# Deeper look-ahead and moved gradient blocks ahead of a backward loop

## The chip, the cores and the metric

The kernel runs on one core of a Trainium2 chip. The metric is the time of one execution in device microseconds. Seven executions of the kernel before took 5657.28 to 5668.17 us, with a median of 5661.39 us.

## What is computed

The reference is one training step, forward and backward, of a block with a memory-augmented attention (A) and a gated feed-forward part (B):

```
xn = layernorm(x)                      # x: 2048 tokens of 640
s  = A(xn);  g = silu(B(xn));  out = x + s * g
A: mem = mem0                          # 8 rows
   for each of 64 segments of 32 tokens:
       h = [mem ; xs]                  # 40 rows
       q, k, v = h Wq, h Wk, h Wv      # 32 heads of 128
       p = softmax(mask(q k^T / sqrt(128)));  o = (p v) Wo
       mem = o[:8];  out rows = o[8:]
B: out = (silu(x w1) * (x w3)) w2
```

The outputs are `out` and the gradients of x, mem0 and the seven weights for a given `grad_out`. All arrays are bf16. The memory rows link the segments, so the forward pass of A is a chain of 64 steps, and the backward pass is a chain of 64 steps in the other direction, from step 63 to step 0.

## The kernel before

The kernel is a sequence of stages that pass their data through scratch tensors in HBM. The ones that matter here are the end of the forward pass of A, the output stage, and the beginning of its backward pass.

**Tiles and units.** Three segments make one tile: 24 memory rows and 96 token rows, 120 in all. There are 22 tiles; the last (tile 21) holds one segment, 8 + 32 = 40 rows. A unit is one tile and four heads (`qd`, 512 columns), so a tile has eight units.

**phase3b_out (L814, the output stage).** It multiplies the attention's rows with Wo (`ld`, `turn`, `proj`, L834 to L865). Its work is 32 turns, four blocks of eight: two blocks of three tiles, then tile 20, then tile 21. In a turn, the rows of the turn four later are loaded (`orow`, five buffers, on SP's queue), the next turn's rows are transposed on PE, and this turn's are multiplied. Two other things ride along. The first is `fetch` (L822 to L826, issued at L920): 13 loads of weights that the backward pass needs, five of 1 MB (WoT) and eight of 1.28 MB (WvT and WkT), one a turn on SP's queue behind the turn's row load. The second is `gox` (L894): gradient units. One such unit takes 128 tokens of the scaled output gradient (`g0x`, loaded from GST) and makes 512 columns of their product with WoT: five matmuls of 512 columns into one PSUM bank, a copy to SBUF (DVE for even units, ACT for odd ones), and after every second unit a store of 128 x 1024 to the scratch tensor GX0 from ACT's queue. GX0 holds tokens 1344 to 2047, so there are six blocks of eight units, 48 in all, from the last token block to the first. They are taken from turn 7 on, one a turn in the first two blocks of turns and three a turn after that.

**phase4_Abwd (L960, the backward pass).** For each unit it has six functions. `ld` (L1131) loads a unit's q and v rows (`gqv`: the memory rows of q and of v in one or two pieces each, and the token rows of both), its output gradients (`gor`, from GX0 for tiles 14 to 21), and its probabilities (`gPr`). `turn` transposes v and the gradients on PE, copies them out on ACT (`gvT`, two buffers, and `gOT`) and stores gvT to VTD from POOL's queue. `dprob` multiplies the two. `dsoft` makes the softmax gradient on DVE (`gdS`) and stores it to DSR from POOL's queue. `gmem` multiplies for the keys and values of the memory rows, copies on ACT (`gks`) and stores to GXP from SP's queue. `gmem_ld` is `gmem` followed by the load of a further unit.

The lead-in (L1256 to L1271) runs 19 units ahead of the first step: the eight of tile 21 (40 rows, called small below), the eight of tile 20 and three of tile 19 (120 rows, called big). It is a software pipeline: iteration i does `turn` of unit i, `dprob` and `dsoft` of unit i-1, and `gmem_ld` of unit i-2. Four loads go out ahead of it, into four buffers, so the load behind `gmem` of unit i-2 is that of unit i+2. `gor` and `gPr` are issued from ACT's queue, the rest from SP's. In iterations 1, 4, 7 and 10 POOL issues a quarter of WqT, 1.28 MB each. The last four loads are those of units that belong to the steps. At the end SP issues the loads of step 63 (vTt, gPm, Qst, krow, xp, gride), and POOL copies gride into the input of the step's first matmuls (L1003).

Then `chain(t)` runs for t = 63 to 0, with the remaining units of the tiles placed into its gaps by hand.

**What sets the order.** Both stages end with `in_order`, which makes every engine keep the order in which the program wrote its instructions. An instruction that waits therefore holds up all that is written behind it on its engine or queue. DMAs are issued by SP, ACT and POOL, each with a queue of its own.

Of the kernel before, what the change touches and what calls it, by code (L numbers as in the profile page):

```python
# [9 lines left out]
BF16 = mybir.dt.bfloat16  # L10
F32 = mybir.dt.float32
# [5 lines left out]
P = 128  # L17
# [23 lines left out]
class K:  # L41
# [110 lines left out]
    def setup_dram(self):  # L152
        tc = self.tc
        S, D, T, H, F = self.S, self.D, self.T, self.H, self.F
        HD = self.HD
        dp = self.ctx.enter_context(tc.tile_pool(name="scratch", bufs=1, space=bass.MemoryType.DRAM))
        self.dp = dp
        mk = lambda name, shape, dt=BF16: dp.tile(list(shape), dt, name=name, uniquify=False)
        self.XN = mk("XN", (S, D))
        self.XNT = mk("XNT", (D, S))  # L160
        self.SLT = mk("SLT", (F, S))
        self.DUT = mk("DUT", (F, S))
        self.HB = mk("HB", (S, F))
# [24 lines left out]
        self.GB0 = 1344  # L188
        self.GX0 = mk("GX0", (S - self.GB0, HD))
# [621 lines left out]
    return Wo  # L811


def phase3b_out(k, Wo, W0, W4):  # L814


    nc, tc = k.nc, k.tc
    D, DC, H, HD, T = k.D, k.DC, k.H, k.HD, k.T
    WT = {}
    WoT = W0.tile([P, DC, HD], BF16, name="WoT", tag="w0")  # L820
    src = k.WOT.rearrange("(dc p) j -> p dc j", p=P)
    fetch = [(WoT[:, dc], src[:, dc]) for dc in range(DC)]  # L822
    for (nm_, src, tag) in (("v", k.WVT, "w1"), ("k", k.WKT, "w2")):
        WT[nm_] = W4.tile([P, H, D], BF16, name=f"W{nm_}T", tag=tag)
        src = src.rearrange("(h p) d -> p h d", p=P)
        fetch += [(WT[nm_][:, h0:h0 + 8], src[:, h0:h0 + 8]) for h0 in range(0, H, 8)]  # L826
    with tc.tile_pool(name="oio", bufs=1) as io, tc.tile_pool(name="oac", bufs=1, space=bass.MemoryType.PSUM) as pa, \
# [5 lines left out]
        st, acc = {}, {}  # L833
# [49 lines left out]
            nc.scalar.dma_start(k.SR[96 * (tl + t):96 * (tl + t) + nx, :], s_tok[0:nx, :])  # L883


        g0 = [(x0, cg, b) for x0 in range(k.GB0, k.S, P)[::-1] for cg in range(4) for b in range(2)]

        def gox_ld(x0):
            w = min(P, k.S - x0)
            xs = io.tile([P, DC, P], BF16, name="g0x", tag="g0x", bufs=2)  # L890
            nc.scalar.dma_start(xs[:, :, 0:w], k.GST[:, x0:x0 + w].rearrange("(dc p) t -> p dc t", p=P))
            st["gx", x0] = xs

        def gox(x0, cg, b):  # L894
            w = min(P, k.S - x0)
            if cg == 0 and b == 0 and x0 > k.GB0:
# [3 lines left out]
            xs, sg = st["gx", x0], st["gs"]  # L900
            c0 = cg * 1024 + b * 512
            pb = ps.tile([P, 512], F32, name="g0pb", tag="opt")
            for dc in range(DC):
                nc.tensor.matmul(pb[0:w, :], xs[:, dc, 0:w], WoT[:, dc, c0:c0 + 512], start=(dc == 0), stop=(dc == DC - 1))
            k.copy(sg[0:w, b * 512:(b + 1) * 512], pb[0:w, :], eng='vs'[b])
            if b == 1:
                nc.scalar.dma_start(k.GX0[x0 - k.GB0:x0 - k.GB0 + w, cg * 1024:(cg + 1) * 1024], sg[0:w, :])

        start = len(nc.cur_bb.bb.instructions)
        assert g0[0][0] - g0[-1][0] == P * (len(g0) // 8 - 1)  # L910
# [5 lines left out]
        for i, (b, qd) in enumerate(work):  # L916
            if i + 4 < len(work):
                ld(*work[i + 4])
            if fetch:
                nc.sync.dma_start(*fetch.pop(0))  # L920
            if i + 1 < len(work):
                turn(*work[i + 1])
            proj(b, qd)
            if late:
                rows_out(*late.pop(0))
            if qd == 7:
                ep_a(b)
# [14 lines left out]
    for s in range(3):  # L942
        t0 = (2, 0, 1)[s]
        n = (T - 1 - t0 + 2) // 3
# [15 lines left out]
def phase4_Abwd(k, out2, WoT, WvT, WkT, WqT, later):  # L960
    nc, tc = k.nc, k.tc
    D, DC, S, H, HD, T = k.D, k.DC, k.S, k.H, k.HD, k.T
    out2f = out2.flatten_outer_dims()
    with tc.tile_pool(name="gst", bufs=1) as st, tc.tile_pool(name="gchain", bufs=1) as ch, \
# [3 lines left out]
        NG = 4  # L968
# [234 lines left out]
        start = len(nc.cur_bb.bb.instructions)  # L1203
# [3 lines left out]
        pro = [(tl, qd) for tl in (k.NTL - 1, k.NTL - 2) for qd in range(8)] + parts[0]  # L1207
        batch = {}
        for i, p in enumerate(parts[1:]):
            batch[T - 2 - i] = p  # L1210

        todo = [u for t in range(T - 1, -1, -1) for u in batch.get(t, ())]

        def ld_next():
            if todo:
                n0 = len(pro) - (total - len(todo))
                ld(*todo.pop(0), nc.scalar if n0 > 0 else nc.sync)

        def gmem_ld(tl, qd):
            gmem(tl, qd)  # L1220
            ld_next()
# [35 lines left out]
        total = len(todo)  # L1257
        for _ in range(4):
            ld_next()
        for i in range(len(pro) + 2):  # L1260
            for f, o in ((turn, 0), (dprob, 1), (dsoft, 1), (gmem_ld, 2)):
                if 0 <= i - o < len(pro):
                    f(*pro[i - o])
            if i % 3 == 1 and i < 12:
                h0 = 8 * (i // 3)
                nc.gpsimd.dma_start(WqT[:, h0:h0 + 8], k.WQT.rearrange("(h p) d -> p h d", p=P)[:, h0:h0 + 8])
        loads(T - 1)
        load_k(T - 1)
        load_xp(T - 1)
# [677 lines left out]
```

## Time and profile before

| what | value |
|---|---|
| median of 7 executions | 5661.39 us |
| the profiled execution | 5668.17 us, the slowest of the seven |
| its span in the profile | 5666.5 us |
| PE busy over the span | 5037.3 us, 89% |
| DVE, ACT, POOL busy | 42%, 32%, 27% |
| output stage, rows first loaded to last matmul | 1981.8 to 2118.2 us |
| lead-in, first load issued to step 63's input copied | 2120.7 to 2227.3 us |

How to read it: the profile lists busy time by engine and cuts the span into slices. PE is the matmul engine and PEld its weight loads; PEclk, or the granted clock, is the share of full speed at which PE ran. A group line names a source line, an engine, an operation, the tile written and the tiles read, and how often. A line of waits says which instruction stood idle, what released it, for how long in total, how many times and the longest. A timeline line has a start, a length, the engine, the line, the operation and its count, and in brackets the idle time ahead of it with what ended it. An engine name with a q is its queue that issues DMAs.

### The profile page before, as it was taken

The numbers are of one execution on the slowest core, as the hardware profiler recorded it, in microseconds if no ns is written. First come the engines' busy times: TensorE is split into PE (matmuls) and PEld (weight loads), VectorE is DVE, ScalarE is ACT, GpSimd is POOL, SyncE is SP. The second block draws the span as 40 slices with busy tenths as digits, with TensorE's granted clock in tenths as the row PEclk, the third lists the DMA queues.
The fourth block names the chain that finished last, engine by engine and source line by source line (L and its number), as shares of the span: only waits on it lengthen the run. The fifth ranks groups of instructions, "written<-read, shape, count | busy, mean of one in ns | idle before, by whom it ended". The sixth has DMA issues, their size and how long they took to land. (4 is left out here: it accounts for less than half of the span.)

```text
span 5666.5 us, 167048 instructions
## 1 busy us (share of the span) xinstructions
PE 5037.3 (89%) x67614; PEld 3209.4 (57%) x67614; DVE 2388.0 (42%) x7479; ACT 1835.4 (32%) x5045; POOL 1551.3 (27%) x2576
## 2 busy tenths in 40 slices
PE   5959799999999784999999997999999999999999
PEld 2536455555555453565556654665566556657565
DVE  5824455555555423444444442332233223311451
ACT  2424355555555522333333331332233122301111
POOL 0000144444444302333333332332234223300000
PEclk9969899999999796999999998999999999999999
DMA  6565355555555475666666664543344334456332
GB/s 219 167 243 197 114 156 160 156 160 160 157 151 149 107 207 155 172 176 175 183 173 178 177 172 108 134 96 93 80 118 99 96 86 106 119 165 227 101 117 91
DMA packets 1009114, 835.81 MB, mean 148 GB/s; under 512 B 506462, under 2 KB 895874, under 8 KB 1005028
## 3 DMA queue, kind: packets, MB, share of 16 engines
q1 hardware_dynamic: 759999, 574.71, 36.6%
q0 software_dynamic: 90352, 141.70, 8.9%
q10 hardware_dynamic: 157993, 108.73, 6.7%
q8 instruction: 533, 8.73, 0.7%
q14 instruction: 237, 1.94, 0.1%
HBM read 511.81 MB, written 324.39 MB: 148 GB/s over the span
## 5 line engine op out<-in xcount | busy, mean ns | idle before, releaser
L1409 PE MATMUL wg<-gr,hr 120*128 120x512 bf16 (+1 forms) x2640 | 591.6, 385 | 17.6 <-DVE dST L1341 13.1
L1387 PE MATMUL g<-w,gT 128*128 128x320 bf16 x3840 | 547.8, 299 | 0.0
L1409 PEld LDWEIGHTS <-hr 120*128 120x128 bf16 (+1 forms) x2640 | 258.5, 99 | 342.6 <-issue 50.7
L1387 PEld LDWEIGHTS <-gT 128*128 128x128 bf16 x3840 | 368.6, 98 | 136.0
L250 POOL DMA_DIRECT2D r<-GOS x256 | 143.4, 564 | 792.3 <-PE r6p L1351 749.4
L373 PEld LDWEIGHTS <-gkv 128*8 128x8 bf16 x8192 | 217.7, 100 | 159.7 <-DVE gkv L1048 35.0
L90 DVE CAST wgo<-wg 128x512 bf16<-128x512 f32 x72 | 47.5, 687 | 586.6 <-PE wg L1409 294.0
L354 PEld LDWEIGHTS <-hx 128*32 128x32 bf16 x7680 | 177.6, 96 | 164.0 <-issue 3.3
L373 PE MATMUL gbank<-WvT,gkv 128*8 128x320 bf16 x4096 | 236.5, 410 | 28.0 <-DVE gkv L1048 28.0
L90 DVE CAST stg<-bank 128x512 bf16<-128x512 f32 x256 | 176.9, 691 | 199.6 <-PE bank L354 188.8
L663 ACT ACTIVATE xP<-xsp,xnm 120x120 bf16<-120x120 f32 (+1 forms) x704 | 239.9, 375 | 10.4 <-DVE xnm L659 5.2
L1396 DVE TENSOR_TENSOR ghacc<-ghacc,g 128x320 f32<-128x320 f32 x240 | 116.9, 487 | 277.1 <-PE g L1387 277.1
L92 ACT CAST wgo<-wg 128x512 bf16<-128x512 f32 x48 | 25.8, 589 | 639.2 <-PE wg L1409 639.2
L1354 ACT CAST gr<-r6p 120x512 bf16<-120x512 f32 (+1 forms) x176 | 103.1, 586 | 351.4 <-PE r6p L1351 337.9
L1185 POOL DMA_DIRECT2D DSR<-gdS x176 | 100.5, 571 | 409.1 <-DVE gdS L1183 386.8
L92 ACT COPY gT<-t6g 128x960 bf16<-128x960 bf16 (+5 forms) x216 | 166.8, 792 | 128.0 <-PE t6g L1370 127.6
L712 POOL DMA_DIRECT2D OR<-xv x163 | 94.1, 577 | 407.5 <-ACT xv L711 290.2
L674 POOL TENSOR_TENSOR xP<-xP,xrz 120x480 bf16<-120x480 bf16 x163 | 161.7, 992 | 140.1 <-ACT xP L663 91.0
L1183 DVE SCALAR_TENSOR_TENSOR gdS<-gdp,Dx,gPr 120x120 bf16<-120x120 f32 (+1 forms) x704 | 188.6, 329 | 0.0
L1180 DVE CUSTOM_DVE_ANT_0 gdS<-gdp,gPr 120x120 bf16<-120x120 f32 (+1 forms) x704 | 153.6, 273 | 65.2 <-PE gdp L1169 54.8
L1155 POOL DMA_DIRECT2D VTD<-gvT x176 | 129.3, 738 | 180.2 <-ACT gvT L1154 155.7
L1370 PE MATMUL t6g<-ident,gr 120*128 120x120 bf16 (+1 forms) x2112 | 172.3, 221 | 3.3 <-DVE wgo L90 2.7
(340 smaller groups left out, 11218.0 us busy)
## 6 DMA issues: line engine op xcount, KB each, us to landing
QVS<-stg SPq DMA_DIRECT2D x128, 256.0 KB
gqv<-QVS SPq DMA_DIRECT2D x112, 192.0 KB
vTt<-VTD SPq DMA_DIRECT2D x64, 320.0 KB
VTD<-gvT POOLq DMA_DIRECT2D x168, 120.0 KB, 3.4
OR<-xv POOLq DMA_DIRECT2D x163, 120.0 KB, 2.6
DSR<-gdS POOLq DMA_DIRECT2D x168, 112.5 KB, 3.3
dS<-DSR SPq DMA_DIRECT2D x168, 112.5 KB
P<-PR SPq DMA_DIRECT2D x168, 112.5 KB
```

The lines of the kernel that those rows point to most:

```text
L90: return nc.vector.tensor_copy(out, in_)
L92: return nc.scalar.copy(out, in_)
L250: eng.dma_start(d, src if src.shape[0] > 1 else src[0])
L354: k.nc.tensor.matmul(bank[32 * g:32 * g + 32, :], x[:, dc, :], W[:, dc, c0:c0 + 512], start=(dc == 0), stop=(dc == k.DC - 1), tile_positio ...
L373: k.nc.tensor.matmul(pm[p0:p0 + nq, 0:320], x[:, h, :], W[:, h, 320 * b:320 * b + 320], start=(first and i == 0), stop=(last and i == 15), ...
L663: nc.scalar.activation(Pb[0:n, j, 0:n], sp[0:n, j, :], ACT.Exp, bias=nmx[0:n, j:j + 1], scale=k.scale, accum_out=Z[0:n, j:j + 1])
L674: eng.tensor_tensor(Pb[0:n, :, 0:n], Pb[0:n, :, 0:n], bc_last(rz[0:n], n), ALU.mult)
L1180: nc.vector.tensor_tensor_reduce(dS[0:n, j, :], dp[0:n, j, :], Pr[0:n, j, :], 1.0, 0.0, ALU.mult, ALU.add, Dx[0:n, j:j + 1])
L1183: nc.vector.scalar_tensor_tensor(dS[0:n, j, :], dp[0:n, j, :], Dx[0:n, j:j + 1], Pr[0:n, j, :], op0=ALU.subtract, op1=ALU.mult)
L1370: nc.tensor.transpose(pt[:, i - i0, j, :], st["g", u, i][0:n, j * P:(j + 1) * P], k.ident[0:n, 0:n])
L1387: nc.tensor.matmul(pg[:], ring[:, i, j, r0:r0 + P], Ws[qd][i][:, j, 320 * h:320 * h + 320], start=(i == 0 and j == 0), stop=(i == 2 and j ...
L1409: nc.tensor.matmul(accs[dc][:], hr[0:n, tl, dc * P:(dc + 1) * P], st["g", NTL * qd + tl, i][0:n, :], start=(tl == 0), stop=(tl == NTL - 1))
```

## The change

Three things are changed; the rest of the program is as it was, apart from line numbers.

The first is in the output stage. The last two blocks of gradient units (tokens 1344 to 1599, 16 units) are not made there; 32 units remain. And of the 13 weight fetches the first five still go out one a turn, but the other eight only in every third turn: turns 6, 9, 12, 15, 18, 21, 24 and 27.

The second is the loads of the lead-in. Six go out ahead instead of four. Units whose number is 4 or 5 modulo 6 use a new buffer pair, `xb`, in SBUF that `krow` of step 63 takes later; the others use the four buffers of before. So the load behind `gmem` of unit i-2 is that of unit i+4. In the lead-in the memory rows of v are issued from POOL's queue, `gor` from ACT's queue for units after the fourth and from SP's before, and `gPr` from SP's queue. The last four loads, which belong to the steps, stand at the last four iterations, as before.

The third is where the 16 units went: one at the end of each iteration 1 to 16 of the lead-in, after that iteration's WqT fetch if it has one. They use the banks bA and bB, which the steps use later; the block load (at the first of eight units, right before its matmuls, in the one buffer that `xp` takes later) and the stores (one buffer, that of `gstg`) are on POOL's queue.

```diff
+def gx_ld(k, xs, x0, eng):
+    w = min(P, k.S - x0)
+    eng.dma_start(xs[:, :, 0:w], k.GST[:, x0:x0 + w].rearrange("(dc p) t -> p dc t", p=P))
+
+def gx_block(k, xs, sg, pb, WoT, x0, cg, b, eng):
+    w = min(P, k.S - x0)
+    c0 = cg * 1024 + b * 512
+    for dc in range(k.DC):
+        k.nc.tensor.matmul(pb[0:w, :], xs[:, dc, 0:w], WoT[:, dc, c0:c0 + 512], start=(dc == 0), stop=(dc == k.DC - 1))
+    k.copy(sg[0:w, b * 512:(b + 1) * 512], pb[0:w, :], eng='vs'[b])
+    if b == 1:
+        eng.dma_start(k.GX0[x0 - k.GB0:x0 - k.GB0 + w, cg * 1024:(cg + 1) * 1024], sg[0:w, :])
...
-        g0 = [(x0, cg, b) for x0 in range(k.GB0, k.S, P)[::-1] for cg in range(4) for b in range(2)]
+        g0 = [(x0, cg, b) for x0 in range(k.GB0 + k.GL, k.S, P)[::-1] for cg in range(4) for b in range(2)]
...
-            if fetch:
+            if fetch and (len(fetch) > 8 or i % 3 == 0):
                 nc.sync.dma_start(*fetch.pop(0))
...
-        def ld(tl, qd, eng=nc.sync):
+        def ld(tl, qd, eng=None):
             ns, nm, nx, n = k.geo(tl)
             c0, h0 = qd * 512, qd * 4
-            qv = fl.tile([120, 2, 512], BF16, name="gqv", tag="gqv", bufs=4)
-            k.load_m(qv, tl, "qv", c0, c0 + 512, nc.sync)
+            i = cnt["l"]
+            cnt["l"] += 1
+            early = i < len(pro)
+            g = i % 6 if early else (i - len(pro) + 1) % NG
+            if g < NG:
+                gor = gors[g][:]
+                qv = fl.tile([120, 2, 512], BF16, name="gqv", tag="gqv", bufs=4)[:]
+                Pr = fl.tile([120, 4, n], BF16, name="gPr", tag="gPr", bufs=4)[:]
+            else:
+                x = xb[:, g - NG]
+                qv = x[:, 0:1024].rearrange("p (i c) -> p i c", i=2)
+                gor = x[:, 1024:1536]
+                Pr = x[:, 1536:1536 + 4 * n].rearrange("p (h c) -> p h c", h=4)
+            if gnm.get(g, 0 if g < NG else 1) != 0 and (g >= NG or gnm[g] < nm):
+                nc.vector.memset(gor[0:24, :], 0.0)
+            gnm[g] = nm
+            for (a, b, src, w) in k.m_src(tl, "qv", c0, c0 + 512):
+                (nc.gpsimd if early and w else nc.sync).dma_start(qv[a:b, w], src if src.shape[0] > 1 else src[0])
             k.load_x(qv, nm, k.x_src(tl, "qv", c0, c0 + 512), nc.sync)
-            gor = gors[qd % NG]
-            if tl == k.NTL - 2 and qd < NG:
-                nc.vector.memset(gor[0:24, :], 0.0)
-            k.load_x(gor, nm, k.g_src(tl, c0, c0 + 512), eng)
-            Pr = fl.tile([120, 4, n], BF16, name="gPr", tag="gPr", bufs=4)
-            eng.dma_start(Pr[0:n], k.PR[tl][:, h0:h0 + 4, :])
+            k.load_x(gor, nm, k.g_src(tl, c0, c0 + 512), nc.scalar if early and i > 3 else nc.sync)
+            nc.sync.dma_start(Pr[0:n], k.PR[tl][:, h0:h0 + 4, :])
...
+        xb = ch.tile([120, 2, 2048], BF16, name="xb", tag="krow", bufs=1)
+        g0 = [(x0, cg, b) for x0 in range(k.GB0, k.GB0 + k.GL, P)[::-1] for cg in range(4) for b in range(2)]
+
+        def gox(x0, cg, b):
+            if cg == 0 and b == 0:
+                uu["gx"] = ch.tile([P, DC, P], BF16, name="gx0", tag="xp", bufs=1)
+                gx_ld(k, uu["gx"], x0, nc.gpsimd)
+            if b == 0:
+                uu["gs"] = ch.tile([P, 1024], BF16, name="gstg", tag="gstg", bufs=1)
+            gx_block(k, uu["gx"], uu["gs"], (bA, bB)[b], WoT, x0, cg, b, nc.gpsimd)
+
-        for _ in range(4):
+        for _ in range(6):
             ld_next()
         for i in range(len(pro) + 2):
-            for f, o in ((turn, 0), (dprob, 1), (dsoft, 1), (gmem_ld, 2)):
+            for f, o in ((turn, 0), (dprob, 1), (dsoft, 1), (gmem, 2)):
                 if 0 <= i - o < len(pro):
                     f(*pro[i - o])
+            if 0 <= i - 2 and (i - 2 + 6 < len(pro) or i >= len(pro) - 2):
+                ld_next()
             if i % 3 == 1 and i < 12:
                 h0 = 8 * (i // 3)
                 nc.gpsimd.dma_start(WqT[:, h0:h0 + 8], k.WQT.rearrange("(h p) d -> p h d", p=P)[:, h0:h0 + 8])
+            if g0 and i > 0:
+                gox(*g0.pop(0))
```

`GB0` is 1344 and `GL` is 256. The output stage's own `gox` calls `gx_ld` and `gx_block` with ACT's queue.

More of the change, by code (lines that the diff above doesn't have):

```diff
@@ L188, in setup_dram @@
         self.GB0 = 1344
+        self.GL = 2 * P
         self.GX0 = mk("GX0", (S - self.GB0, HD))
@@ L883, in rows_out @@
             nc.scalar.dma_start(k.SR[96 * (tl + t):96 * (tl + t) + nx, :], s_tok[0:nx, :])
-        g0 = [(x0, cg, b) for x0 in range(k.GB0, k.S, P)[::-1] for cg in range(4) for b in range(2)]
+        g0 = [(x0, cg, b) for x0 in range(k.GB0 + k.GL, k.S, P)[::-1] for cg in range(4) for b in range(2)]
         def gox_ld(x0):
-            w = min(P, k.S - x0)
             xs = io.tile([P, DC, P], BF16, name="g0x", tag="g0x", bufs=2)
-            nc.scalar.dma_start(xs[:, :, 0:w], k.GST[:, x0:x0 + w].rearrange("(dc p) t -> p dc t", p=P))
+            gx_ld(k, xs, x0, nc.scalar)
             st["gx", x0] = xs
         def gox(x0, cg, b):
-            w = min(P, k.S - x0)
-            if cg == 0 and b == 0 and x0 > k.GB0:
+            if cg == 0 and b == 0 and x0 > k.GB0 + k.GL:
                 gox_ld(x0 - P)
@@ L899, in gox @@
                 st["gs"] = io.tile([P, 1024], BF16, name="g0st", tag="g0st", bufs=3)
[L900 to L907, printed above, removed]
+            gx_block(k, st["gx", x0], st["gs"], ps.tile([P, 512], F32, name="g0pb", tag="opt"), WoT, x0, cg, b, nc.scalar)
         start = len(nc.cur_bb.bb.instructions)
@@ L1129, in phase4_Abwd @@
         uu = {}
-        def ld(tl, qd, eng=nc.sync):
+        gnm = {}
+        def ld(tl, qd, eng=None):
             ns, nm, nx, n = k.geo(tl)
             c0, h0 = qd * 512, qd * 4
-            qv = fl.tile([120, 2, 512], BF16, name="gqv", tag="gqv", bufs=4)
-            k.load_m(qv, tl, "qv", c0, c0 + 512, nc.sync)
-            k.load_x(qv, nm, k.x_src(tl, "qv", c0, c0 + 512), nc.sync)
-            gor = gors[qd % NG]
-            if tl == k.NTL - 2 and qd < NG:
-                nc.vector.memset(gor[0:24, :], 0.0)
-            k.load_x(gor, nm, k.g_src(tl, c0, c0 + 512), eng)
-            Pr = fl.tile([120, 4, n], BF16, name="gPr", tag="gPr", bufs=4)
-            eng.dma_start(Pr[0:n], k.PR[tl][:, h0:h0 + 4, :])
+            i = cnt["l"]
[16 more added lines that the diff above has]
+                (nc.gpsimd if early and w else nc.sync).dma_start(qv[a:b, w], src if src.shape[0] > 1 else src[0])
+            k.load_x(qv, nm, k.x_src(tl, "qv", c0, c0 + 512), nc.sync)
+            k.load_x(gor, nm, k.g_src(tl, c0, c0 + 512), nc.scalar if early and i > 3 else nc.sync)
+            nc.sync.dma_start(Pr[0:n], k.PR[tl][:, h0:h0 + 4, :])
             uu["l", tl, qd] = qv, gor, Pr
@@ L1210, in phase4_Abwd @@
             batch[T - 2 - i] = p
+        cnt = dict(l=0)
         todo = [u for t in range(T - 1, -1, -1) for u in batch.get(t, ())]
@@ L1215, in ld_next @@
             if todo:
-                n0 = len(pro) - (total - len(todo))
-                ld(*todo.pop(0), nc.scalar if n0 > 0 else nc.sync)
+                ld(*todo.pop(0))
         def gmem_ld(tl, qd):
@@ L1256, in phase4_Abwd @@
         todo = pro + todo
-        total = len(todo)
-        for _ in range(4):
+        xb = ch.tile([120, 2, 2048], BF16, name="xb", tag="krow", bufs=1)
[8 more added lines that the diff above has]
+        for _ in range(6):
             ld_next()
         for i in range(len(pro) + 2):
-            for f, o in ((turn, 0), (dprob, 1), (dsoft, 1), (gmem_ld, 2)):
+            for f, o in ((turn, 0), (dprob, 1), (dsoft, 1), (gmem, 2)):
                 if 0 <= i - o < len(pro):
                     f(*pro[i - o])
+            if 0 <= i - 2 and (i - 2 + 6 < len(pro) or i >= len(pro) - 2):
+                ld_next()
             if i % 3 == 1 and i < 12:
@@ L1266, in phase4_Abwd @@
                 nc.gpsimd.dma_start(WqT[:, h0:h0 + 8], k.WQT.rearrange("(h p) d -> p h d", p=P)[:, h0:h0 + 8])
+            if g0 and i > 0:
+                gox(*g0.pop(0))
+        assert not g0
         loads(T - 1)
```

## The prediction, made before the changed kernel was run

> **What bounds the kernel now.** I first read the slices of the page and then tables of 8 us stretches, to find the part that the change touches. The forward chain ends at about 1980 us. The output stage (phase3b_out) runs from 1982 to 2118 us, the lead-in of the backward pass (19 units, then the set-up of step 63) from 2121 to 2227 us, and the 64 backward steps follow. Columns: stretch, length, busy time of PE, PEld, DVE, ACT and POOL, granted clock, DMA share, GB/s.
>
> ```profile
> 2040.00:2048.00 8.00, 6.21 (x52) 4.12 (x51) 0.64 (x2) 1.06 (x2) 0.00 (x0) 1.00 1.12 261
> 2096.00:2104.00 8.00, 8.00 (x77) 4.02 (x75) 2.06 (x5) 2.44 (x4) 0.00 (x0) 1.00 0.40 125
> 2168.00:2176.00 8.00, 1.59 (x24) 1.52 (x24) 3.34 (x22) 1.65 (x7) 2.98 (x5) 0.50 0.86 264
> 2192.00:2200.00 8.00, 2.70 (x37) 2.43 (x35) 3.00 (x23) 2.45 (x9) 2.55 (x4) 0.50 0.65 195
> ```
>
> There are three regimes. Until about 2057 us the DMA engines are full and PE has gaps; from there to 2118 us PE is full and the DMA engines are at 0.4; in the lead-in neither is full and PE stands idle two thirds of the time at half clock. So the question there is a latency. The waits of PE name it, first in the output stage, then in the lead-in (us in total, times, longest):
>
> ```profile
> PE opt L853 <- DMA orow<-OR: 9.2, 7, 1.9
> ```
>
> ```profile
> PE gvpt L1151 <- DMA gqv<-QVS: 45.1, 12, 8.5
> PE gbank L354 <- POOL gox L1003: 16.7, 1, 16.7
> ```
>
> The timeline of PE (start, length) shows the price of both. Gradient units come three to a turn, 15 matmuls, with no gap; in the lead-in big units come in pairs 2 us apart and then wait 5 to 6 us:
>
> ```profile
> 2096.08 3.40 PE L904 MATMUL g0pb<-WoT,g0x 128*128 128x512 bf16 x15
> 2099.41 0.26 PE L853 MATMUL opt<-ident,orow 32*128 32x32 bf16 x4
> ...
> 2188.93 0.56 PE L1151 MATMUL gvpt<-ident,gqv 120*128 120x120 bf16 x4 [4.98 <-DMA gqv<-QVS]
> 2190.56 0.56 PE L1151 MATMUL gvpt<-ident,gqv 120*128 120x120 bf16 x4
> 2197.64 0.56 PE L1151 MATMUL gvpt<-ident,gqv 120*128 120x120 bf16 x4 [5.13 <-DMA gqv<-QVS]
> ```
>
> **The change part by part. 1, gradient units leave the output stage.** 48 units become 32. They are taken one a turn from turn 7 and three a turn from turn 16, so turn 23 loses one and turns 24 to 28 lose all 15. There PE is full, and one unit takes 3.33/3 = 1.11 us (2096.08 to 2099.41). 16 x 1.11 = **-17.7 us**, all on the path.
>
> **2, the weight fetches are spread.** Before, one 1.28 MB fetch per turn goes out in turns 5 to 12; these turns last 6.0 us with PE busy 78%. Afterwards a turn of this kind holds 0.29 MB of rows, 0.13 MB of stores and a third of a fetch, 0.84 MB in about 4.4 us, 190 GB/s against the 295 GB/s that the stage moved while full. The 9.2 us of PE's waits should go; I count **-8** (bounds -9.2 and -4, as the 5.2 MB of WoT in turns 0 to 4 stay bunched). The whole stage moves 28.9 - 2.4 = 26.5 MB, 90 us at 295 GB/s, so it doesn't become the bound of a stage of 112 us.
>
> **3, what is late next.** Turns 24 to 31 then hold no gradient units and last 0.8 us each (2115.56 to 2116.35), while the last two fetches go out in turns 24 and 27. The row loads of turns 29 to 31 stand behind 1.28 MB on SP's queue, 4.4 us at 295 GB/s, and the four turns of lead are worth 3.2 us plus landing. I take **+4** (bounds 0 and 2 x 4.4 = 8.8). The output stage: -17.7 - 8 + 4 = -21.7.
>
> **4, the start of the lead-in.** The value rows of the first units now come through POOL, after its memset and mask (0.6 us), each 0.55 us to issue and 2.9 to 3.4 to land by the rows of POOL's own stores, so the first turn is some 4.5 us after the pool is free instead of 3.7: **+0.8** (bounds 0, +2). The later five queue there ahead of the first VTD store, 2.8 us, which ends before that store is due.
>
> **5, the body, first turn to the key/value product of unit 15.** It lasts 2124.4 to 2202.4 = 78.0 us. Loads go out two iterations ahead and return after about 6.5 us, hence pairs every 8.6 us. Six units in flight are four iterations ahead, and the wait for gqv should mostly go. What then holds an iteration? PE: 1.6 us for a small unit (2127.59 to 2129.16) and 1.6 to 2.2 for a big one, plus a gradient unit, 1.1 at full clock and twice that at the half clock shown, so 2.7 to 4.4. DVE about 2.4 (four times 0.21 spacing, four at 0.27, half a 0.69 copy, some of the ten 0.27 us memsets). POOL about 2.7: stores of 0.7 and 0.55, a row load 0.6, half a store of gradients, a quarter of a 0.92 us fetch issue. Transfers: 14.5 MB now, 16.9 with the two blocks, 57 us at 295 GB/s against 183 GB/s reached now. I take 3.5 us an iteration, 17 x 3.5 = 59.5.
>
> To this come two new waits of PE, which loads each block just where it uses it. The first load stands on POOL's queue right behind the first 1.28 MB fetch of WqT, which takes 9.1 us to land; that this queue holds up what follows is in ACT's timeline, where gvT of the fifth unit waits for a VTD store issued behind that fetch:
>
> ```profile
> 2139.53 0.18 ACT L1153 COPY gvT<-gvpt 128x32 bf16<-128x32 bf16 x1 [8.44 <-DMA VTD<-gvT]
> ```
>
> I price it at 9. The second is issued on POOL behind a DSR store that waits for DVE, and behind no fetch: 6 (bounds 3.4, the landing of a store, and 9). Behind PE's waiting matmul stand the next unit's transposes, and behind these ACT, DVE and both stores. Sum 59.5 + 15 = 74.5, **-3.5**. Bounds: 57 + 3 = 60 (-18), and 4.4 x 9 + 3.8 x 8 + 15 + 6 (delays behind the three later fetches) = 91 (+13).
>
> The Trainium skill, "DMA: Bandwidth & Descriptors", section "Issuing engines are not separate DMA queues", speaks against one part: transfers from SP, ACT and POOL share the same engines, and more issuers save only issue time. The trace leaves this open here, since the lead-in is below the full rate; by the rule three queues are worth nothing beyond the deeper look-ahead, which is also how I priced them, and the sum stays.
>
> **6, the end.** From the store after unit 15 to step 63 there are 24.6 us, held by SP: four units of loads for the steps, 3.4 us of issue each, then vTt to gride (2218.9 to 2223.3) and gride's landing at 2227. The changed program has these four units at the same place, so 0. SP no longer loads anything in the two iterations ahead of it; nothing of that is on the path.
>
> **At nothing:** six memsets more (DVE is a third busy in this stretch); Pr's issue moved from ACT to SP (0.37 us, SP has room at 3.5 us an iteration); the copies (0.69 DVE, 0.59 ACT); krow waiting for the extra buffers, last read two iterations before the lead-in ends and needed in step 63 only; the gradient store that must land before the next copy on DVE: 0.6 + 3.4 us within two iterations of 7. At iterations under 3 us this cover is gone, and up to 1 us per pair comes back, 8 in all.
>
> Sum: -21.7 + 0.8 - 3.5 = **-24.4 us**. The profiled execution took 5668.17 us (span 5666.5), the slowest of the seven, so it would become 5643.8; against the median 5661.39 that is **5637.0**.
>
> **Rivals.** *A, the lead-in flows too:* PE warms up with the added work, iterations fall to 2.7 us and the block waits to 9 together: body 60, -18. Output stage at its bound -27. Together -32 to -45: 5616 to 5629. For it: no engine is over 2.7 us; against it: four 1.28 MB fetches on the queue that now also carries loads. *B, POOL's queue holds the body:* every WqT fetch delays stores and now value rows, the body grows by 4 to 16, and 5 to 17 are left: 5644 to 5656. *C, slower than before:* the same queue as a serial chain, iteration by iteration (gradient matmuls, ACT's copy, POOL's store, the next unit's VTD store behind it, its landing, the buffer of gvT that ACT needs two units on). It takes the place of the load wait; with 17 such rounds at 4.6 us now it decides from (78 + 21)/17 = 5.8 us, and at the 6.6 us spacing seen after a fetch (2133.47 to 2139.84) the body is 112: 5674. Against it: VTD lands in 3.8 us when no fetch is ahead. *D, the spread doesn't do what it says:* the rows wait behind fetches in the short turns as they do now in the long ones, both bounds of part 3, and POOL adds some: -5 to -12, 5650 to 5656.
>
> **How the numbers follow.** Forecast (5629 to 5643) 0.54, A 0.18, B 0.16, C 0.05, D 0.07. A range of 5616 to 5654 takes in the forecast, A and most of B. A measurement tells 0.2%, 11.3 us, from no change, so faster means below 5650.1: forecast, A and half of B, 0.80; C with 0.01 of accidents is slower, 0.06; the other half of B and D stay within, 0.14.
>
> **What would show it.** Output stage: PE's wait for orow below 2 us before turn 24, some 4 after it, the stage 22 us shorter. Lead-in: the wait for gqv from 45 to below 15, waits for the block loads of about 9 and 6 in its place, DMA above 220 GB/s; end to step 63 unchanged at 24 to 25 us. Wrong if the end of the lead-in isn't SP's, if the stores' landing times on POOL's queue pass 7 us, or if the output stage keeps waiting for rows in turns 8 to 16.

## The result, and the profile after

The changed kernel takes 5642.39 us (median of 15 executions, 5627.02 to 5664.99) against 5661.39 before (37 executions, 5645.8 to 5672.85). The ratio is 0.9966, 95% interval 0.9957 to 0.9975: 19 us less, between 14 and 24. The forecast of 5637.0 was 5.4 us too low; the sign and the range were right. How the time came about was not: by the profiles, the output stage's half of the sum holds to a microsecond, the lead-in's is out by 17 us.

The profiled execution took 5659.27 us, span 5657.4; it is one of the slowest of this kernel. I cut the traces into three. The **output stage** runs from the first `opt` matmul to the end of the last one. The **lead-in** runs from there to the copy of `gride` on POOL, with which step 63 has its input. **Behind** is the rest of the span. For each kernel there is a second profile, from one more execution.

| us | before | before, again | after | after, again |
|---|---|---|---|---|
| output stage | 132.6 | 134.1 | 110.0 | 108.8 |
| lead-in | 108.8 | 110.1 | 123.0 | 124.6 |
| both | 241.4 | 244.2 | 233.0 | 233.4 |
| behind step 63's input | 3439.5 | 3438.8 | 3436.6 | 3431.0 |

Both stages repeat within 1.6 us in these two pairs, so I read differences of 3 us and more between single profiles. The output stage lost 22.6 us and the lead-in gained 14.2: **two thirds of what the first gives, the second takes back.**

The waits of PE in the output stage, the changed kernel (us in total, times, longest; 9.2, 7, 1.9 before):

```profile
PE opt L870 <- DMA orow<-OR: 3.6, 4, 1.8
```

The timeline of PE (start, length) at the end of that stage. The last gradient unit ends at 2090.9, and the short turns follow each other every 0.79 us without a gap, although the last two fetches went out in turns 24 and 27:

```profile
2088.62 2.32 PE L825 MATMUL g0pb<-WoT,g0x 128*128 128x512 bf16 x10
2090.88 0.26 PE L870 MATMUL opt<-ident,orow 32*128 32x32 bf16 x4
...
2093.55 0.26 PE L870 MATMUL opt<-ident,orow 32*128 32x32 bf16 x4
2093.74 0.67 PE L881 MATMUL sT<-oT,Wo 128*128 128x32 bf16 x20
2094.34 0.26 PE L870 MATMUL opt<-ident,orow 32*128 32x32 bf16 x4
```

Now the waits of PE in the lead-in. The wait for `gqv` fell from 45.1 to 7.8 us, as meant. Two others stand in its place. The kernel before has no wait for `gx`, and its wait for `gdS` is the first line here; the lines below it are the changed kernel's, of which the third is the end, as before (16.7):

```profile
PE gkp L1195 <- DVE gdS L1183: 1.4, 3, 0.9
```

```profile
PE gbank L825 <- DMA gx<-GST: 23.4, 2, 11.9
PE gkp L1217 <- DVE gdS L1205: 20.2, 7, 9.0
PE gbank L355 <- POOL gox L1011: 16.5, 1, 16.5
PE gvpt L1173 <- DMA gqv<-QVS: 7.8, 2, 6.3
```

The table of stretches of the changed kernel (stretch, length, busy PE, PEld, DVE, ACT, POOL, granted clock, DMA share, GB/s) shows both halves. In the output stage the DMA engines are full until 2040 us, as before, but no longer after it (share 1.12 before, 0.36 now), and PE is nearly full. In the lead-in there are holes of 8 us in which PE does next to nothing while the DMA engines move 201 to 268 GB/s:

```profile
2040.00:2048.00 8.00, 7.78 (x64) 5.18 (x62) 1.07 (x3) 1.06 (x2) 0.00 (x0) 1.00 0.36 84
...
2112.00:2120.00 8.00, 0.32 (x1) 0.13 (x2) 0.00 (x0) 0.00 (x0) 1.81 (x2) 0.50 0.66 201
2152.00:2160.00 8.00, 0.00 (x0) 0.00 (x0) 0.70 (x3) 0.00 (x0) 2.88 (x5) 0.57 0.84 268
```

These two holes are the waits for the two blocks. POOL issued the first block's load at 2113.16, 0.9 us behind the WqT fetch of 2112.24, and it took 6.5 us to land:

```profile
2113.16 0.89 POOL L817 DMA_DIRECT2D gx<-GST  x1
```

```profile
2119.68 2.31 PE L825 MATMUL gbank<-WoT,gx 128*128 128x512 bf16 x5 [11.49 <-DMA gx<-GST]
```

The wait for `gdS` can be read off the same queue. The timeline of POOL shows what it issues: a WqT fetch of 1.28 MB, and 0.9 us later a store of a pair of gradient units.

```profile
2133.06 0.96 POOL L1301 DMA_DIRECT2D WqT<-WQT  x1
2133.99 0.58 POOL L828 DMA_DIRECT2D GX<-gstg  x1
```

The timeline of DVE says when that store had landed. The next copy needs the one buffer `gstg`; it waits until 2141.87, 7.9 us after the issue, and once more behind the fetch of 2169.74. The store landed at 2141.8, 0.8 us after the fetch ahead of it (2140.9). Where no fetch is ahead the landing takes 2.8 to 3.5 us and the copy waits 2.7 to 2.8:

```profile
2141.87 0.69 DVE L90 CAST gstg<-gbank 128x512 bf16<-128x512 f32 x1 [7.85 <-DMA GX<-gstg]
2148.11 0.69 DVE L90 CAST gstg<-gbank 128x512 bf16<-128x512 f32 x1 [2.77 <-DMA GX<-gstg]
2179.53 0.69 DVE L90 CAST gstg<-gbank 128x512 bf16<-128x512 f32 x1 [9.14 <-DMA GX<-gstg]
```

Behind that copy on DVE stands `dsoft` of the next unit, behind its `gdS` the `gmem` matmuls on PE: that is most of the line of 20.2 us (4.4 and 9.0 us behind the two late stores). The second block load is held by a fetch in another way: by the profile's releaser, POOL stood 4.76 us before it could issue it, until the WqT fetch of 2147.38 had landed, and PE then waited for the block:

```profile
2158.76 0.92 POOL L817 DMA_DIRECT2D gx<-GST  x1 [4.76 <-DMA WqT<-WQT]
```

```profile
2162.70 2.31 PE L825 MATMUL gbank<-WoT,gx 128*128 128x512 bf16 x5 [11.91 <-DMA gx<-GST]
```

The second profile has the same stand (3.86 us), experiments 2 and 6 too (3.05 and 3.47), but experiment 7, with fewer DMAs on POOL's queue, has none. Why POOL stands there, no run shows.

### The profile page after: what moved, and what is told of

Same layout as the page of the kernel before. It is cut to its first block, busy times and chain, and to the rows that moved or that the text cites. A ratio compares the mean times of both kernels' runs of the same rounds, so it can differ in the third digit from the quotient of the medians.

```text
span 5657.4 us, 167071 instructions
## 1 busy us (share of the span) xinstructions
PE 5042.0 (89%) x67614; PEld 3203.5 (57%) x67614; DVE 2389.9 (42%) x7485; ACT 1835.3 (32%) x5045; POOL 1569.9 (28%) x2605
## 5 line engine op out<-in xcount | busy, mean ns | idle before, releaser
L675 POOL TENSOR_TENSOR xP<-xP,xrz 120x480 bf16<-120x480 bf16 x163 | 161.7, 992 | 140.0 <-ACT xP L664 93.3
L539 DVE COPY vt<-stg 8x512 bf16<-8x512 bf16 x512 | 165.2, 323 | 20.9 <-ACT stg L92 13.4
L1177 POOL DMA_DIRECT2D VTD<-gvT x176 | 130.5, 743 | 148.9 <-ACT gvT L1176 125.9
```

The source lines that it names most:

```text
L539: nc.vector.tensor_copy(vt[p0:p0 + 8, c0:c0 + 512], sv[32 * g:32 * g + 8, b * 512:(b + 1) * 512])
L675: eng.tensor_tensor(Pb[0:n, :, 0:n], Pb[0:n, :, 0:n], bc_last(rz[0:n], n), ALU.mult)
```

## The experiments

**Theory.** The gain is the output stage's. The lead-in loses because the two blocks were put on POOL's queue, behind the WqT fetches, are loaded where they are used, and have one staging buffer. **Rivals.** The spread fetches make the gain and the moved units do nothing; the lead-in is held by the rate of all transfers, whatever the queue; it is held by the value rows on POOL's queue; or six units in flight do not matter. All ratios are against the kernel before; "us" beside a ratio is the ratio applied to 5661.4. Stage times are from one profile each.

**1. The spread alone.** On the kernel before:

```diff
-            if fetch:
+            if fetch and (len(fetch) > 8 or i % 3 == 0):
```

> The kernel before with one line changed: the last eight weight fetches of the output stage go out every third turn instead of every turn; all 48 gradient units stay in the output stage and the lead-in is as before. Theory (the gain is made in the output stage, 22.7 us of it in the profiled pair, of which 16 units x 1.11 = 17.7 were the moved units, so that 5.0 are the spread): this kernel is 5 us below the kernel before (3 to 8), and its output stage 127 to 128 us instead of 132.6. Rival (the spread is what matters, the moved units only fill gaps): 15 to 20 below. Rival (the spread only moves the wait for rows to other turns): within 2 us.

Measured: 5652.47 us, ratio 0.9989 (0.9979 to 0.9998), 6 us less (1 to 12). Output stage 125.9, lead-in 111.2. The stage lost 6.7 us (8.2 against the second profile of before), a little more than expected. By the stage the theory holds and both rivals fall; the total alone, 1 to 12, would not settle the second of them. PE's wait for the rows is nearly gone (9.2 before):

```profile
PE opt L853 <- DMA orow<-OR: 1.3, 2, 0.7
```

**2. The changed kernel without the spread** (the diff above, reversed).

> The changed kernel with the fetches of the output stage unspread again, one a turn as before. Theory: the spread's 5 us come back, so 14 us below the kernel before (11 to 17), output stage 115 us, PE's wait for the rows back at 9 us. Rival (with 16 units fewer the stage is not full of work and the rows are what bounds it, so the spread is worth more than alone): 9 us below the kernel before or less.

Measured: 5657.69 us, ratio 0.9987 (0.9976 to 0.9997), 7 us less (2 to 14). Output stage 115.1 as expected, PE's wait for the rows 7.3 (expected 9), lead-in 125.8. So the moved units alone shorten the stage by 132.6 - 115.1 = 17.5 us, and the spread on top by 5.1. The total is below the 11 to 17 expected; the lead-in is 17.0 us longer than before, 2.8 more than in the changed kernel. With 240.8 for both stages against 241.4, this kernel has gained nothing up to step 63.

**3. Block loads and gradient stores on ACT's queue.**

```diff
-                gx_ld(k, uu["gx"], x0, nc.gpsimd)
+                gx_ld(k, uu["gx"], x0, nc.scalar)
...
-            gx_block(k, uu["gx"], uu["gs"], (bA, bB)[b], WoT, x0, cg, b, nc.gpsimd)
+            gx_block(k, uu["gx"], uu["gs"], (bA, bB)[b], WoT, x0, cg, b, nc.scalar)
```

> The changed kernel with the two block loads and the eight gradient stores of the lead-in issued by ACT instead of POOL, so that they no longer stand on POOL's queue behind the 1.28 MB fetches of WqT. Theory (the queue): the staging copy on DVE and ACT no longer waits 8 to 9 us twice, the first block lands in 4 to 5 us instead of 6.6 after issue and the second doesn't wait for a fetch to land; the body of the lead-in goes from 93 to about 75 us, and the kernel to 10 to 18 us below the changed kernel. Rival (transfers share the same 16 engines, so the queue they are issued on is worth only the issue time): within 2 us of the changed kernel, with the same waits for gstg and for the blocks. Rival (ACT is in the chain, two more issues of 0.9 us a pair delay gvT): slower by 2 to 8.

Measured: 5634.68 us, ratio 0.9951 (0.9938 to 0.9963), 28 us less than before (21 to 35). The lead-in falls from 123.0 to 109.3; PE's wait for `gdS` from 20.2 to 5.8 us, and the first block's from 11.5 to 2.7. Who issues these ten DMAs is worth 13.7 us here. Of this the shorter issues are some 2.7 us (0.34 us for a store instead of 0.57, 0.45 for a load instead of 0.90); the rest is the queue and POOL's stand before the second load, which this edit moves together. The rival of the 16 shared engines falls as a statement about this lead-in, but not wholly: the second block, with no fetch ahead of it on ACT's queue, still comes late. The waits of PE (this line names `gqv`; the weight load of the same block waited 10.0 for `gx`), and the stretch it falls into, with the DMA engines full:

```profile
PE gbank L825 <- DMA gqv<-QVS: 10.3, 1, 10.3
```

```profile
2136.00:2140.00 4.00, 0.00 (x0) 0.00 (x0) 1.89 (x13) 0.83 (x4) 2.13 (x4) 0.50 0.96 321
2140.00:2144.00 4.00, 0.00 (x0) 0.00 (x0) 0.00 (x0) 0.00 (x0) 0.00 (x0) 0.50 1.04 337
```

The loads of the units ahead, a fetch and the block were asked for at once, and the block is needed first.

**4. All 48 units back in the output stage,** the rest as changed (`self.GL = 0` for `2 * P`).

> The changed kernel with all 48 gradient units back in the output stage; six units in flight, three queues and the spread fetches stay. Theory (the lead-in is lost to the moved blocks and their transfers, not to the six units in flight): the output stage is 127.5 us, the lead-in falls clearly below the 106 us of the kernel before, to 85 to 95 us, since the wait for gqv goes and nothing takes its place; so 16 to 25 below the kernel before. Rival (value rows on POOL's queue behind the fetches, or the fetches themselves, hold the body whatever the blocks do): lead-in 104 to 115 us, and 0 to 7 below the kernel before.

Measured: 5640.91 us, ratio 0.9964 (0.9952 to 0.9976), 20 us less (14 to 27). Output stage 125.8, lead-in 99.0, 9.8 below the kernel before. The lead-in is slower than the 85 to 95 I expected: something does take the place of the wait for `gqv`, and it is the same queue again, VTD stores of the units behind fetches (landing after 6.5 to 10.4 us there, 1.8 to 5.2 elsewhere). The waits of ACT, and of PE behind it:

```profile
ACT gvT L1175 <- DMA VTD<-gvT: 43.3, 10, 11.0
```

```profile
PE ggpt L1180 <- ACT gvT L1176: 28.1, 4, 8.7
```

This run shows what moving the blocks was worth: the output stage is 15.8 us longer without it and the lead-in 24.0 shorter. The ratio is that of the changed kernel. **As it was placed, the move brought nothing** (by the stages it cost 8 us); the look-ahead with its queues and the spread, without the move, give the whole of the 19 us.

**5. WqT in sixteen fetches instead of four.**

```diff
-            if i % 3 == 1 and i < 12:
-                h0 = 8 * (i // 3)
-                nc.gpsimd.dma_start(WqT[:, h0:h0 + 8], k.WQT.rearrange("(h p) d -> p h d", p=P)[:, h0:h0 + 8])
+            if 1 <= i < 17:
+                h0 = 2 * (i - 1)
+                nc.gpsimd.dma_start(WqT[:, h0:h0 + 2], k.WQT.rearrange("(h p) d -> p h d", p=P)[:, h0:h0 + 2])
```

> The changed kernel with the four WqT fetches of 1.28 MB in the lead-in split into sixteen of 0.32 MB, one an iteration, on the same queue (POOL). Theory (what POOL issues stands behind a whole fetch on its queue): the gradient stores, block loads, VTD stores and value rows then wait for at most 0.32 MB, about 2 to 3 us, instead of 8 to 11; the staging copies no longer wait 8 to 9 us, the lead-in goes from 123 to 105 to 112 us and the kernel to 10 to 18 below the changed one. Rival (it isn't the queue, it is the transfer rate of all 16 engines, the same bytes take the same time): lead-in 118 to 125, the kernel within 3 us. Rival (twelve more issues of 0.9 us on POOL): slower by up to 10.

Measured: 5644.4 us, ratio 0.9969 (0.9959 to 0.9979), no difference from the changed kernel; lead-in 120.0. My theory missed, and the number is the rival's. Still, the rate is not what holds the stage: experiments 3 and 8 move the same bytes in less time. The trace offers another reason: a fetch now stands ahead of every gradient store. Landing times of the gradient stores (min, median, max), first in the changed kernel and then here, and DVE's wait here (25.2, 5 in the changed kernel):

```profile
DMA to landing us min/median/max: 2.8/5.6/8.8
```

```profile
  DVE gstg L90: 30.3, 6
...
DMA to landing us min/median/max: 4.0/4.8/5.4
```

DVE's longest wait shrinks from 9.1 to 6.1 us, the number of waits grows, and PE's wait for `gdS` stays at 20.1. Here splitting what stands ahead did not help what stands behind each piece.

**6. Four units in flight instead of six** (`range(4)` for `range(6)` ahead of the loop, `i - 2 + 4` for `i - 2 + 6` in it).

> The changed kernel with four units in flight instead of six (blocks, queues and spread as changed). Theory: the depth is what took away the wait for gqv, 45 us before and 8 after; with four units it comes back, though partly in the shadow of the block and staging waits, so that the lead-in grows by 10 to 25 us over 123. Rival (with the blocks in the lead-in an iteration lasts 5 us and more anyway, four units cover the loads): within 4 us of the changed kernel.

Measured: 5649.53 us, ratio 0.998 (0.997 to 0.9989), 11 us less than before (6 to 17); lead-in 126.2. The lead-in is only 1.6 to 3.2 us above the two profiles of the changed kernel, as the rival had it, though the total is some 7 us above, with intervals that overlap. The waits of PE show one wait passing into another: `gqv` is back, `gdS` is gone (20.2 in the changed kernel):

```profile
PE gvpt L1173 <- DMA gqv<-QVS: 25.4, 9, 6.2
PE gbank L825 <- DMA gx<-GST: 23.5, 2, 12.1
...
PE gkp L1217 <- DVE gdS L1205: 1.3, 2, 0.9
```

With the blocks on POOL's queue the depth is worth little in the lead-in; without them the deeper look-ahead and its queues together gave 9.8 us (experiment 4). No run takes these two apart.

**7. Value rows on SP's queue.**

```diff
-                (nc.gpsimd if early and w else nc.sync).dma_start(qv[a:b, w], src if src.shape[0] > 1 else src[0])
+                nc.sync.dma_start(qv[a:b, w], src if src.shape[0] > 1 else src[0])
```

> The changed kernel with the value rows of the early units on SP's queue again (two queues instead of three). Theory: the value rows on POOL's queue stand behind the fetches and make the units late, and SP has room, so the kernel is the same or up to 6 us faster. Rival, from the Trainium skill, DMA: Bandwidth & Descriptors, section Issuing engines are not separate DMA queues (more issuers save only issue time): within 2 us. Rival (the third queue starts the lead-in sooner and relieves SP, which has some 2.9 us of issue an iteration): slower by 3 to 10 us.

Measured: 5640.08 us, ratio 0.9964 (0.9952 to 0.9976); lead-in 119.5. Two queues do as well as three: the total is the same within the interval, the lead-in 3.5 us shorter. The third queue for these rows brought nothing, and their place on POOL's queue cost little.

**8. All three waits taken away.** Both blocks are loaded at the start into the room of `vTt`, two staging buffers take turns, loads and stores are ACT's, the fetches are sixteen (as in 5):

```diff
-                uu["gx"] = ch.tile([P, DC, P], BF16, name="gx0", tag="xp", bufs=1)
-                gx_ld(k, uu["gx"], x0, nc.gpsimd)
+                uu["gx"] = gxs[x0]
...
-                uu["gs"] = ch.tile([P, 1024], BF16, name="gstg", tag="gstg", bufs=1)
-            gx_block(k, uu["gx"], uu["gs"], (bA, bB)[b], WoT, x0, cg, b, nc.gpsimd)
+                uu["gs"] = ch.tile([P, 1024], BF16, name="gstg", tag=("gstg", "xp")[cg % 2], bufs=1)
+            gx_block(k, uu["gx"], uu["gs"], (bA, bB)[b], WoT, x0, cg, b, nc.scalar)
+
+        gxt = ch.tile([P, 2, DC, P], BF16, name="gx0", tag="vTt", bufs=1)
+        gxs = {}
+        for j, x0 in enumerate(range(k.GB0, k.GB0 + k.GL, P)[::-1]):
+            gxs[x0] = gxt[:, j]
+            gx_ld(k, gxs[x0], x0, nc.scalar)
```

> The changed kernel with all three suspected waits taken away together: both gradient blocks loaded at the start of the lead-in into a buffer of their own (the room that vTt takes later), two staging buffers in turn, block loads and gradient stores issued by ACT, and the WqT fetches split into sixteen on POOL. Theory: no wait for gbank's inputs and none over 3 us for gstg is left, the 17 iterations are held by PE at half clock or by the transfers, the lead-in is 85 to 95 us (123 changed, 109 before) and the kernel 28 to 38 us below the changed one. Rival (the transfer rate holds it: 16.9 MB at 295 GB/s and an end of 24): lead-in 95 to 103, the kernel 20 to 27 below.

Measured: 5624.52 us, ratio 0.994 (0.9927 to 0.9953), 34 us less than before (27 to 41), 18 below the changed kernel by the medians. Lead-in 96.2: 26.8 shorter, 1.2 above my range and within the rival's; the total is short of both, 18 where 28 to 38 and 20 to 27 stood. PE has no wait for `gx` any more, and 0.6 us in all behind a gradient store. What is left is what my theory and the rival named, one after the other. The stretches:

```profile
2104.00:2112.00 8.00, 7.67 (x70) 3.53 (x70) 3.73 (x28) 2.25 (x13) 3.61 (x6) 0.50 0.59 148
...
2128.00:2136.00 8.00, 6.99 (x76) 4.57 (x76) 4.87 (x27) 3.27 (x11) 5.35 (x10) 0.80 1.00 288
2136.00:2144.00 8.00, 4.30 (x41) 2.28 (x41) 3.98 (x24) 3.53 (x11) 5.35 (x9) 0.84 1.00 306
2144.00:2152.00 8.00, 5.15 (x59) 2.74 (x58) 5.45 (x29) 3.53 (x11) 5.01 (x8) 0.94 1.00 293
```

From 2104 to 2120 us PE is nearly full at the half clock and the DMA engines are not. From 2128 us on the DMA engines are full at 288 to 306 GB/s and PE has gaps again. The body lasts some 63 us, to the last matmul of unit 15, close to the lower bound of 60 that the prediction worked out from 295 GB/s.

**9. As 8, with the four large fetches.**

> As e10_early_two_buf, but with the four WqT fetches of 1.28 MB as in the changed kernel. Theory (with blocks and gradient stores off POOL's queue, only the VTD stores and value rows stand behind a fetch there, and they do delay the units: 28 us of such waits were seen in e4_no_blocks_in_lead): lead-in 6 to 12 us longer than the 96.2 of e10_early_two_buf, 102 to 108, the kernel 5 to 12 above it. Rival (six units in flight cover a fetch, so size doesn't matter any more): within 2 us of e10_early_two_buf.

Measured: 5626.12 us, ratio 0.9933 (0.9921 to 0.9944), 38 us less (32 to 45). The lead-in is 101.7, 5.5 above experiment 8, just short of the 6 to 12 expected, while the totals do not differ. On the size of the fetches this is inconclusive. On the rest it is not: against experiment 3 (109.3) early blocks and the second buffer are worth 7.6 us in the lead-in.

**10. As 8, and the loads for the steps behind step 63's inputs.**

```diff
-            if 0 <= i - 2 and (i - 2 + 6 < len(pro) or i >= len(pro) - 2):
+            if 0 <= i - 2 and i - 2 + 6 < len(pro):
                 ld_next()
...
         ride(T - 1)
+        for _ in range(4):
+            ld_next()
```

> As e10_early_two_buf, and the loads of the four units of the backward steps, 3.8 us of issue each on SP, go out behind the inputs of step 63 instead of ahead of them. Theory (the end of the lead-in is SP's issue, the step of the prediction that priced it at 24.6 us): the lead-in falls by 11 to 15 us from 96.2, to 81 to 85, and the kernel by the same, to 47 to 53 us below the kernel before. Rival (the last units' stores or their landing hold the end): by 0 to 4 us. Rival (the step units are late in the first steps): lead-in shorter, but the kernel within 3 us of e10_early_two_buf.

Measured: 5610.69 us, ratio 0.9905 (0.9889 to 0.992), 54 us less than before (45 to 63). This is the fastest kernel of the case. The lead-in is 88.4, 7.8 below experiment 8, where I had expected 11 to 15; the total fell by 14 (medians of 4 and 6 executions), and no run shows where the other 6 us lie. The step units are not late enough to cost what was gained, so that rival falls. POOL's wait for `gride`, first in experiment 8, then here:

```profile
POOL gox L1011 <- DMA gride<-GST: 17.3, 1, 17.3
```

```profile
POOL gox L1011 <- DMA gride<-GST: 8.5, 1, 8.5
```

So SP's issue did hold the end, but not alone: without the step loads SP spends 11.8 us on the last six GXP stores (2164.7 to 2176.5), which wait for their units.

**11 and 12. Both kernels once more,** for second profiles.

> The changed kernel once more, for a second profile. The first one gained 8.4 us from the output stage to step 63 where the medians differ by 19. If that profile's lead-in was typical: output stage 109 to 111, lead-in 122 to 124 us again, and what is missing lies behind step 63. If its waits vary from run to run: lead-in 112 to 118 us.

> The kernel before once more, for a second profile. If its first profile was typical: output stage 131 to 134, lead-in 108 to 110 us. If the missing 10 us are the kernel before having longer stages in other runs: lead-in or output stage 5 to 10 us longer.

Measured: 5652.52 and 5666.39 us in one execution each; the stages are in the first table. Both first profiles were typical, so the two stages account for 8.4 to 10.8 us and not for 19 (the spans differ by 9.1 and 14.0). The span behind step 63's input is 2 to 8.5 us shorter in the changed kernel, where its code does the same. But experiment 1, whose code there is that of before, has 3431.6 against 3439.5, and experiment 5 has 3414.5; so this stretch varies by that much without an edit in it. The time of an execution goes with its mean granted clock: the changed kernel had 0.941 in its two longest executions (5664.99 us, and the profiled one) and 0.946 to 0.947 in its three shortest (5627.02 to 5630.93), and the profile of experiment 5 has 0.945 where those of the kernel before have 0.939 and 0.942. Which of the two causes the other, if either does, no run shows. Whether the changed kernel gains there is open, as is what is then left of the 19 us, whose interval begins at 14.

## Why the prediction was right, and where it was wrong

The forecast was right in sign and nearly in size. Two of its steps, 1 and 2, are why the sign was right. One, step 5, failed by more than its bound, and that the size came out all the same is luck: the two stages gained 8.4 to 10.8 us where the sum had 24.4, and the rest of the 19 is time that the sum does not contain.

**1, units out of the output stage, -17.7: right.** 17.5 alone (experiment 2), 15.8 on top of the spread (4).

**2, the spread, -8: right in mechanism, a little too large.** -6.7 to -8.2 alone, -5.1 after the units had gone. The trace still has 3.6 us of waits: 0.6 in turn 1 and 3.1 in turns 7 to 9 (2009 to 2020 us), where the DMA engines were still full (share 1.05 to 1.12) with the first fetches behind WoT's. The prediction had asked for less than 2.

**3, row loads late behind the last fetches, +4: wrong.** The tail runs without a gap; the lower bound, 0, was it. Steps 1 to 3 together gave -22.6 where -21.7 was forecast: two terms too large by about 3 us together cancel one that did not come.

**4, the start, +0.8: not seen.** 3.2 to 3.4 us from the first load to the first turn, 3.7 before.

**5, the body, -3.5, bounds -18 and +13: this step failed.** The body, first turn to the store behind the product of unit 15, took 93.3 us instead of 78.0, +15.3, above the upper bound. By its own terms: the block waits, priced at 9 + 6, were 11.5 + 11.9; the second load was priced as behind no fetch, and the trace shows POOL waiting for one. Another 16.4 us of PE's waits for `gdS` lie in the body (the other 3.9 of the 20.2 come after unit 15), and most of them, 4.4 + 9.0, came from an item in **"At nothing"**: the gradient store that must land before the next copy was costed at 0.6 + 3.4 us, the landing on a free queue, with a cover of 7 us. Two of the eight stores stood right behind a fetch, and landed after 7.8 and 8.8; a third, 4.1 us behind one, took 8.5, but the next copy was waiting for the second block by then. The rest, 93.3 - 23.4 - 16.4 = 53.5 us, is 3.1 an iteration instead of 3.5. The very line that I quoted for the block load, ACT waiting 8.44 us for a store issued behind a fetch, applied to these stores as well, and I did not apply it.

**6, the end, 0: right.** 23.4 us, 24.6 before, and SP's in part: without the step loads the lead-in is 7.8 us shorter (experiment 10).

Of the signs that the prediction named, a stage 22 us shorter, a wait for `gqv` below 15 and an unchanged end came. Not so the DMA rate, 180 GB/s over the body instead of above 220; and stores landing after more than 7 us on POOL's queue, which it had named as a sign of being wrong, came too.

Rival B, POOL's queue holding the body with a growth of 4 to 16 us, is what happened in the lead-in (+15.3, and 13.7 back when the blocks leave the queue). The time that it gave, 5644 to 5656, holds what the profiled stages alone would make of the median before (5661.4 - 8.4 = 5653.0); the measured median lies 2 us below. Its value rows had no part in it (experiment 7). The rival C's chain, every iteration waiting, was not seen: ACT waited 0.4 us in all for a VTD store, and PE's waits for `gdS` without a fetch ahead were 2.4 us at most.

The page on DMA had been weighed against the third queue: the Trainium skill, "DMA: Bandwidth & Descriptors", section "Issuing engines are not separate DMA queues". For the value rows the runs agree with it (experiment 7, no difference). For the blocks they do not: the same ten transfers moved to another queue shortened the lead-in by 13.7 us (experiment 3), far over the some 2.7 us of issue time saved.

## What to carry to other kernels

Before you put a small transfer on a queue, list what stands ahead of it there, and price it with the landing of the large one, also where nothing seems to wait for a store: its buffer does. Work moved into idle engine time is free only if its loads and stores are free too; give it a load ahead of time, two buffers and a queue without bulk fetches, and only then count the time it leaves behind. When a wait disappears and the stage is no shorter, read the new list of waits: here `gqv` turned into `gx` and `gdS`, without the blocks into `gvT`, and last into PE at half clock and the transfer rate.

## What the runs showed of the hardware

A transfer of 0.26 MB took 2.8 to 3.5 us to land from POOL's queue and 7.8 to 8.8 us behind 1.28 MB on it. Sixteen fetches of a quarter of the size made that 4.0 to 5.4 for every store whose landing the profile tells.

The granted clock stayed at half through long stretches of a busy PE; the prediction had left open whether a moved unit takes 1.1 us or twice that. The changed kernel, where the moved units took 2.3 us each against 1.11 in the output stage:

```profile
2120.00:2124.00 4.00, 4.00 (x32) 1.78 (x31) 1.92 (x13) 0.84 (x5) 0.58 (x1) 0.50 0.00 0
2124.00:2128.00 4.00, 4.00 (x32) 1.65 (x30) 1.23 (x12) 1.31 (x6) 2.65 (x5) 0.50 0.38 114
2128.00:2132.00 4.00, 4.00 (x39) 1.79 (x37) 2.10 (x14) 0.98 (x6) 1.36 (x4) 0.50 0.39 107
2132.00:2136.00 4.00, 4.00 (x51) 2.13 (x48) 1.50 (x13) 1.72 (x9) 3.82 (x7) 0.50 0.72 164
```

The profile shows 16 us without a gap on PE at 0.50, though the ends of matmuls are modelled and about 1 us of each 3.3 us is short matmuls; in its second profile PE is busy 3.67 to 4.00 of 4 us in these stretches, also at 0.50. The Trainium skill, "TensorE: Matmul & The Clock Gate", section "What's actually happening", has the full clock after about 3.4 us of sustained work; here the measurement says otherwise, and no run shows why.
